# New instruction prices for the planner that orders all five queues, a price for a wait on one's own engine, turns of VectorE and GpSimd, and the sign of the first MLP's weights set on VectorE

## The chip, the cores and the metric

The kernel runs on one core of a Trainium2 chip. The metric is the device time of one execution in microseconds (us), from the first to the last instruction and the little that lies around it. Five engines work side by side, each through a queue of its own in a fixed order: TensorE (PE in the rows, with its weight loads as PEld), VectorE (DVE), ScalarE (ACT), GpSimd (POOL) and SyncE (SP), which only issues transfers.

## The reference

Top-32 attention over 4 batches, 8 heads, 576 positions and head size 64, then two MLPs in a row over the 2304 resulting tokens, 512 to 2048 to 512 each. All inputs are float32 or wider; the kernel reads the MLPs' weights as pairs of 32-bit words.

```python
scores = scale * np.matmul(q, k.transpose(0, 1, 3, 2))
kth = np.partition(scores, -top_k, axis=-1)[..., -top_k:-top_k + 1]
scores = np.where(scores >= kth, scores, -1000000000.0)
scores = scores - np.max(scores, axis=-1, keepdims=True)
attn = np.exp(scores); attn = attn / (np.sum(attn, axis=-1, keepdims=True) + 1e-09)
x = np.matmul(attn, v)            # then (batch, seq, heads * head_dim)
h = x @ w_in;   x = (np.maximum(h, 0.0) + np.log1p(np.exp(-np.abs(h)))) @ w_out     # first MLP
h = x @ w_in2;  y = (h - np.tanh(h)) @ w_out2                                      # second MLP
```

## The kernel before

Every large product is made from float16 pairs, a high part and a low part of each operand, with three matmuls for one (high by high, high by low, low by high).

Attention is cut into 144 tiles of 128 query rows by 576 scores. For each tile `front` makes the scores on TensorE and copies them to the tile `ssb` on ScalarE. `chain` finds the 32 largest of each row on VectorE: four MAX8 (eight largest values, into `m`) and between them three MATCH_REPLACE8 (write a very small number over those eight, into `x`), each of which needs the one before it; a MATCH_REPLACE8 stands in the trace behind a short MATCH_VALUE_LOAD. `exps`, `mask` and `turn` make the masked exponentials (ScalarE, VectorE, GpSimd), split them into `hl` (ScalarE high part, GpSimd low part) and send them through a transposing transfer to `pT`. `back` multiplies with the values into `px` and normalises (`x32`, `xs`). The chains of two neighbouring tiles are recorded in turns. There are three buffers each of `ssb` and `x`.

The MLPs run over chunks of 256 tokens (two smaller ones of 128). A chunk's first MLP can run when the 16 or more tiles that make its tokens are done. A step is an eighth of the inner width: `gemm1` (PSUM tile `h`), `act1` (ScalarE's softplus or tanh into `r`, for tanh a VectorE instruction more, ScalarE's `g` high part, GpSimd's scaled `r` and low part), `gemm2` (PSUM tiles `y`). In the rows `hinab`, `gsab` belong to the first MLP, `hinb`, `gsb` to the second.

The four weight matrices are turned into float16 pairs in the kernel, in 32 groups (8 of each matrix), the first MLP's 16 groups first. They lie early in the run, beside the first attention tiles. `weight_convert` (line 619) rebuilds magnitudes from the two words; `weight_split` (line 656) sets sign and scale and makes the pair. The tiles of these instructions are called `whi`, `wlo` and `xy` in the rows, after the place where the raw words lie: the rows with 128x1024 are groups in one piece, those with 128x256 are groups in four pieces. All 16 groups of the first MLP are in one piece, and 8 of the second MLP's. With `SGN[i]` "1" a group in one piece costs, in `weight_split`: VectorE one tensor_scalar that puts the scale under the sign bit, GpSimd two multiplications of 512 columns, ScalarE one copy to the high part, GpSimd two subtractions of 512 columns for the low part. With "0" (the `else` branch, there already): VectorE one scalar_tensor_tensor that joins sign and magnitude, ScalarE one activation with the scale to the high part, GpSimd one tensor_scalar of 1024 columns in place (`WSE` is "1"), and the same two subtractions.

No order of instructions is written by hand. The kernel's functions only record operations (class `Recorder`); at the end `order` (line 376) runs a list scheduler, `place` (line 309), over the whole program, five times with ranks improved between, takes the turn with the shortest plan, and issues the operations in that order. Each engine of the plan takes, at the time when it is free, the operation with the lowest rank among those that are ready; when none is ready it moves to the first that gets ready. For TensorE those ready for 500 ns are preferred. A duration comes from `price` (line 219), a delay between dependent operations from `close` (line 270): for another engine's result the producer's latency (100 to 350 ns), for a result of the same engine, or of a transfer, 0. `CON` (0.3) makes a VectorE operation that `two` (line 259) names (more than 8 elements, all inputs in SBUF, no MAX8 or MATCH_REPLACE8) 30% longer when GpSimd is busy at its start, and a GpSimd operation longer by 30% of its overlap with such a one. All of this is issued from one helper, so every row has its line, L402. The scheduler's plan is only an order: on the chip each engine works through its queue in that order and waits at its head for what is late.

Of the kernel before, what the change touches and what calls it, by code (L numbers as in the profile page):

```python
# [27 lines left out]
V2 = 'BD'  # L28
WSE = '1111'
PLAN = '01_23 01_23 01_23 01_23'  # L30
SGN = '1111'
PSB = '0000'
NRM = 'cccc'
EVL = 'AA'
HIC = 'AAAA'
CON = 0.3
SOFT = 1
NKT = 2
NQT = 2
# [98 lines left out]
class Recorder:  # L138
# [80 lines left out]
    def price(self, eng, method, a, k, outs, ins):  # L219
        out = outs[0]  # L220
        n = max(math.prod(x.shape[1:]) for x in outs + ins)
        if eng == "PE":
            cols = math.prod(out.shape[1:])
            if ins[0].dtype == F32:
                return 240 + cols * 4 / 2.4, 350.0
            return max(31.0, cols / 2.4 + 2.5), 350.0
        if eng == "SP":
            size = math.prod(out.shape) * mybir.dt.size(out.dtype)
            if "transpose" in method:
                return 1350.0, size / 164.0  # L230
            return 540.0, size / 330.0
        if eng == "ACT":
            if method == "copy":
                return 90 + 0.82 * n, 160.0
            c = 90 + 0.88 * n
            if len(a) > 2 and a[2] == AF.Exp:
                c += 200
            c += 70 * sum(isinstance(k.get(x), View) for x in ("bias", "scale"))
            return c + (95 if k.get("accum_out") is not None else 0), 160.0
        if eng == "DVE":  # L240
            if method == "max":
                return 705.0, 140.0
            if method == "match_replace":
                return 700.0, 140.0
            if n <= 8:
                return 400.0 if method == "scalar_tensor_tensor" else 120.0, 140.0
            if method == "tensor_reduce":
                return 300.0, 140.0
            far = any(isinstance(x, View) and x.ap.space == bass.MemoryType.PSUM for x in ins)
            if method in ("tensor_scalar", "tensor_copy"):  # L250
                return (70 + 1.1 * n if far else 100 + 0.58 * n), 140.0
            return (50 + 1.3 * n if far else 140 + 1.04 * n), 140.0
        if method == "memset":
            return 100 + 0.4 * n, 100.0
        if method == "tensor_scalar":
            return 270 + 0.84 * n, 100.0
        return 200 + 1.7 * n, 100.0

    def two(self, op):

# [9 lines left out]
    def close(self, op):  # L270
        op.i = len(self.ops)
        self.ops.append(op)

        def need(j):
            if j != op.i:
                o = self.ops[j]
                op.preds[j] = 0.0 if o.eng in (op.eng, "SP") else o.lat

        for mine, both in ((op.reads, False), (op.writes, True)):
            for g, (p0, p1, lo, hi) in mine:  # L280
                if not g.users or g.users[-1] != op.i:
                    g.users.append(op.i)
                for lst in (g.writes, g.reads) if both else (g.writes,):
                    for q0, q1, l, h, j in lst:
                        if q0 < p1 and p0 < q1 and l < hi and lo < h:
                            need(j)
        for g, (p0, p1, lo, hi) in op.writes:
            for lst in (g.reads, g.writes):
                lst[:] = [e for e in lst if not (p0 <= e[0] and e[1] <= p1 and lo <= e[2] and e[3] <= hi)]
            g.writes.append((p0, p1, lo, hi, op.i))  # L290
        for g, (p0, p1, lo, hi) in op.reads:
            g.reads.append((p0, p1, lo, hi, op.i))
# [16 lines left out]
    def place(self, edges, count, rank, margin, ring):  # L309

        ops = self.ops
        left = list(count)
        ready = [0.0] * len(ops)
        start, end = [0.0] * len(ops), [0.0] * len(ops)
        free = dict.fromkeys(("PE", "DVE", "ACT", "POOL", "SP"), 0.0)
        coming = {e: [] for e in free}
        avail = {e: [] for e in free}
        for o in ops:
            if not left[o.i]:
                heapq.heappush(coming[o.eng], (0.0, o.i))  # L320
        two, both = self.wide, 0.0
        done, busy = [], 0.0
        while True:
            best = None
            for e in free:
                if avail[e]:
                    t = free[e]
                elif coming[e]:
                    t = max(free[e], coming[e][0][0])
                else:  # L330
                    continue
                if best is None or t < best[0]:
                    best = t, e
            if best is None:
                break
            t, e = best
            while coming[e] and coming[e][0][0] <= t:
                r, i = heapq.heappop(coming[e])
                heapq.heappush(avail[e], (rank[i], i))
            i = None  # L340
            if margin.get(e):
                aside = []
                while avail[e]:
                    x = heapq.heappop(avail[e])
                    if ready[x[1]] <= t - margin[e]:
                        i = x[1]
                        break
                    aside.append(x)
                for x in aside:
                    heapq.heappush(avail[e], x)  # L350
            if i is None:
                i = heapq.heappop(avail[e])[1]
            o = ops[i]
            start[i] = t
            done.append(o)
            cost = o.cost
            if CON:
                if e == "DVE" and two[i]:
                    if free["POOL"] > t:
                        cost *= 1 + CON  # L360
                    both = t + cost
                elif e == "POOL" and both > t:
                    cost += CON * min(both - t, cost)
            end[i] = free[e] = t + cost
            if ring and e == "SP":
                busy = max(busy, t + 800) + o.lat
                end[i] = busy + 1000
            for j, lat in edges[i]:
                ready[j] = max(ready[j], end[i] + lat)
                left[j] -= 1  # L370
                if not left[j]:
                    heapq.heappush(coming[ops[j].eng], (ready[j], j))
        assert len(done) == len(ops)
        return start, end, done
# [31 lines left out]
def topk_attention_two_mlps(  # L406
# [249 lines left out]
    def weight_split(i, g, parts, used, ss):  # L656
# [8 lines left out]
        for st, cols in parts:  # L665
            low, high = st[:, :, 0], st[:, :, 1]
            w, hi, lo = high.bitcast(F32), whi[i][:, cols], wlo[i][:, cols]
            n = w.shape[1] // LSP if w.shape[1] > 512 else w.shape[1]
            if SGN[i] == "1":
                nc.vector.tensor_scalar(high, high, -0x80000000, s.bitcast(I32), op0=ALU.bitwise_and, op1=ALU.bitwise_or)  # L670
# [850 lines left out]
```

## Time and profile before

| | us |
|---|---|
| median of 3 runs | 1232.31 |
| lowest, highest | 1231.5, 1236.07 |
| the profiled execution, its own time | 1232.63 |
| its span, first to last instruction | 1230.9 |
| VectorE busy in the span | 1015.2 |
| TensorE busy in the span | 1001.5 |
| GpSimd busy in the span | 933.8 |
| ScalarE busy in the span | 906.7 |

The profile is of one execution. Busy times of an engine are the union of its instructions' spans. In the timeline an instruction's span runs some 80 ns into that of the next one on its engine, so the pace of an engine is read from one start to the next, not from the spans. A stretch given in us counts from the first instruction.

### The profile page before, as it was taken

The numbers are of one execution on the slowest core, as the hardware profiler recorded it, in microseconds if no ns is written. First come the engines' busy times: TensorE is split into PE (matmuls) and PEld (weight loads), VectorE is DVE, ScalarE is ACT, GpSimd is POOL, SyncE is SP. The second block draws the span as 40 slices with busy tenths as digits, with TensorE's granted clock in tenths as the row PEclk, the third lists the DMA queues.
The fourth block names the chain that finished last, engine by engine and source line by source line (L and its number), as shares of the span: only waits on it lengthen the run. The fifth ranks groups of instructions, "written<-read, shape, count | busy, mean of one in ns | idle before, by whom it ended". The sixth has DMA issues, their size and how long they took to land.

```text
span 1230.9 us, 27536 instructions
## 1 busy us (share of the span) xinstructions
PE 1001.5 (81%) x9832; PEld 791.0 (64%) x9832; DVE 1015.2 (82%) x2146; ACT 906.7 (74%) x1834; POOL 933.8 (76%) x1282
## 2 busy tenths in 40 slices
PE   2333323587897999888999999999997999999998
PEld 2222222476655876776678876887676768977974
DVE  4999999899998999999999999999898998710011
ACT  7988888867998897768876886799667766733332
POOL 4999998888987965866889868888795778743433
PEclk9999996698899989998999999999999999999999
DMA  8977888724687676634765644456464435210000
GB/s 281 275 231 223 209 220 218 189 76 95 125 177 183 143 177 119 129 73 93 147 128 127 115 93 94 93 117 131 99 132 99 80 74 95 49 23 18 2 3 25
DMA packets 322827, 153.16 MB, mean 124 GB/s; under 512 B 270208, under 2 KB 302464, under 8 KB 322688
## 3 DMA queue, kind: packets, MB, share of 16 engines
q1 hardware_dynamic: 322688, 151.39, 53.8%
q8 instruction: 77, 1.26, 0.4%
q14 instruction: 62, 0.51, 0.1%
HBM read 73.04 MB, written 15.37 MB: 72 GB/s over the span
## 4 chain that ended last, share of the span: by engine, by line
POOL 26%; DVE 24%; PE 23%; ACT 10%; issue 8%; DMA 7%; SPq 1%; POOLq 0%; DVEq 0%; ACTq 0%
PE h L402 11%; PE y L402 10%; DVE m L402 9%; DVE x L402 8%; POOL hl L402 6%; POOL wlo L402 5%; POOL g L402 3%; DMA pT<-hl 3%; POOL x L402 2%; POOL r L402 2%; POOL whi L402 2%; POOL nb L402 2%; ACT x L402 2%; ACT r L402 2%; DMA whi<-in_moe_w_in_dram 1%
## 5 line engine op out<-in xcount | busy, mean ns | idle before, releaser
L402 PE MATMUL h<-xy,whi 128*128 128x256 f16 (+1 forms) x2560 | 406.7, 266 | 4.7 <-DMA xy<-xs 1.7
L402 PEld LDWEIGHTS <-whi 128*128 128x128 f16 x3840 | 360.8, 99 | 67.4 <-issue 10.9
L402 PE MATMUL h<-xy,wlo 128*128 128x256 f16 (+1 forms) x1280 | 329.4, 266 | 0.0
L402 DVE MAX8 m<-x 128x8 f32<-128x576 f32 x432 | 320.4, 753 | 7.2
L402 POOL TENSOR_TENSOR hl<-x,hl 128x512 f16<-128x512 f32 (+1 forms) x288 | 214.6, 764 | 51.4 <-ACT hl L402 42.6
L402 DVE MATCH_REPLACE8 x<-m,x 128x576 f32<-128x576 f32 x288 | 213.4, 741 | 0.0
L402 PE MATMUL y<-g,whi 128*128 128x256 f16 (+1 forms) x1280 | 199.6, 263 | 9.2 <-ACT r L402 5.2
L402 PEld LDWEIGHTS <-wlo 128*128 128x128 f16 x1920 | 189.7, 99 | 25.5 <-issue 5.9
L402 PE MATMUL y<-whi,g 128*128 128x512 f16 x576 | 192.4, 379 | 2.0 <-DVE xy L402 1.5
L402 POOL TENSOR_TENSOR g<-r,g 128x512 f16<-128x512 f32 (+1 forms) x160 | 172.3, 1077 | 20.4 <-PE y L402 9.4
L402 PE MATMUL y<-g,wlo 128*128 128x256 f16 (+1 forms) x640 | 162.9, 263 | 0.0
L402 DVE SCALAR_TENSOR_TENSOR r<-h,hinb,r 128x512 f32<-128x512 f32 (+1 forms) x80 | 55.1, 689 | 124.5 <-ACT r L402 124.2
L402 ACT ACTIVATE x<-ssb,nb,tiny 128x576 f32<-128x576 f32 x144 | 124.3, 865 | 38.0 <-DVE m L402 20.0
L402 PE MATMUL px<-vhl,pT 128*128 128x65 f16 (+1 forms) x2240 | 102.3, 202 | 51.6 <-DMA pT<-hl 25.3
L402 PEld LDWEIGHTS <-pT 128*128 128x128 f16 (+1 forms) x2240 | 94.2, 106 | 72.0 <-DMA pT<-hl 33.8
L402 PE MATMUL s<-kT,qT 128*128 128x288 f16 x512 | 95.3, 315 | 50.0 <-ACT ssb L402 30.7
L402 PEld LDWEIGHTS <-g 128*128 128x128 f16 x864 | 83.1, 98 | 77.5 <-issue 2.1
L402 ACT CAST hl<-x 128x576 f16<-128x576 f32 x144 | 96.4, 670 | 33.7 <-POOL x L402 28.3
L402 DVE MAX8 m<-ssb 128x8 f32<-128x576 f32 x144 | 107.4, 746 | 5.1 <-ACT ssb L402 4.9
L402 PE MATMUL y<-wlo,g 128*128 128x512 f16 x288 | 109.1, 379 | 0.0
L402 DVE MATCH_REPLACE8 x<-m,ssb 128x576 f32<-128x576 f32 x144 | 106.7, 741 | 0.0
L402 POOL TENSOR_SCALAR r<-r,gsb 128x512 f32<-128x512 f32 (+1 forms) x80 | 52.2, 652 | 60.5 <-ACT g L402 58.3
(123 smaller groups left out, 1797.8 us busy)
## 6 DMA issues: line engine op xcount, KB each, us to landing
whi<-in_moe_w_in_dram SPq DMA_DIRECT2D x8, 1024.0 KB, 7.0
wlo<-in_moe_w_in_dram SPq DMA_DIRECT2D x6, 1024.0 KB, 7.0
vd<-vhl SPq DMA_DIRECT2D x16, 330.0 KB, 3.6
vhl<-vd SPq DMA_DIRECT2D x16, 330.0 KB, 3.3
kd<-kT SPq DMA_DIRECT2D x32, 160.0 KB, 2.3
whi<-in_moe_w_out_dram SPq DMA_DIRECT2D x5, 1024.0 KB, 5.7
wlo<-in_moe_w_out_dram SPq DMA_DIRECT2D x5, 1024.0 KB, 5.1
kT<-kd SPq DMA_DIRECT2D x32, 160.0 KB, 2.8
```

The costliest lines, as they stand in the source:

```text
L402: fn(*a, **k)
```

## The change

Four things are changed in the planner, and one in the program.

1. `price`: ScalarE's activations lose 10 ns, its Exp 155 ns more; MAX8 goes from 705 ns to 78 + 1.04 ns a column (677 ns for 576), MATCH_REPLACE8 from 700 to 659 ns; other VectorE operations and GpSimd's get new lines (a GpSimd subtraction of 512 columns goes from 1070 to 1101 ns, its one-column tensor_scalar from 271 to 330 ns, its multiplication of 576 from 1179 to 1360 ns).
2. `turn`, new: an operation that reads or overwrites what an earlier operation of the same engine wrote is ready only some time after that one's end: 116 ns on VectorE (196 ns if it is a MATCH_REPLACE8), 130 ns on ScalarE, 120 ns on GpSimd.
3. `CON` is 0.7 and works both ways: when a VectorE operation that `two` names or a GpSimd operation starts while the other engine is in one, both get longer by 0.7 of the overlap, and what depends on the one already running gets ready later.
4. `place` puts back an operation whose ready time has moved.
5. `SGN` is "0011": the 16 groups of the first MLP take the `else` branch of `weight_split`.

```diff
--- before.py
+++ after.py
@@ -28,12 +28,12 @@
 V2 = 'BD'
 WSE = '1111'
 PLAN = '01_23 01_23 01_23 01_23'
-SGN = '1111'
+SGN = '0011'
 PSB = '0000'
 NRM = 'cccc'
 EVL = 'AA'
 HIC = 'AAAA'
-CON = 0.3
+CON = 0.7
 SOFT = 1
 NKT = 2
 NQT = 2
@@ -232,29 +232,35 @@
         if eng == "ACT":
             if method == "copy":
                 return 90 + 0.82 * n, 160.0
-            c = 90 + 0.88 * n
+            c = 80 + 0.88 * n
             if len(a) > 2 and a[2] == AF.Exp:
-                c += 200
+                c += 45
             c += 70 * sum(isinstance(k.get(x), View) for x in ("bias", "scale"))
             return c + (95 if k.get("accum_out") is not None else 0), 160.0
         if eng == "DVE":
             if method == "max":
-                return 705.0, 140.0
+                return 78 + 1.04 * n, 140.0
             if method == "match_replace":
-                return 700.0, 140.0
+                return 60 + 1.04 * n, 140.0
             if n <= 8:
-                return 400.0 if method == "scalar_tensor_tensor" else 120.0, 140.0
-            if method == "tensor_reduce":
-                return 300.0, 140.0
+                return 350.0 if method == "scalar_tensor_tensor" else 80.0, 140.0
             far = any(isinstance(x, View) and x.ap.space == bass.MemoryType.PSUM for x in ins)
             if method in ("tensor_scalar", "tensor_copy"):
-                return (70 + 1.1 * n if far else 100 + 0.58 * n), 140.0
-            return (50 + 1.3 * n if far else 140 + 1.04 * n), 140.0
+                return (40 + 1.1 * n if far else 130 + 0.53 * n), 140.0
+            return (20 + 1.25 * n if far else 90 + 1.07 * n), 140.0
         if method == "memset":
-            return 100 + 0.4 * n, 100.0
+            return 200 + 0.4 * n, 100.0
         if method == "tensor_scalar":
-            return 270 + 0.84 * n, 100.0
-        return 200 + 1.7 * n, 100.0
+            return 330.0 if n <= 8 else 250 + 0.8 * n, 100.0
+        if method == "tensor_mul":
+            return (220 + 1.98 * n if n > 512 else 200 + 1.57 * n), 100.0
+        return 190 + 1.78 * n, 100.0
+
+    def turn(self, first, then):
+
+        if then.eng == "DVE":
+            return 196.0 if then.calls[0][0].__name__ == "match_replace" else 116.0
+        return {"ACT": 130.0, "POOL": 120.0}.get(then.eng, 0.0)
 
     def two(self, op):
 
@@ -271,10 +277,16 @@
         op.i = len(self.ops)
         self.ops.append(op)
 
-        def need(j):
+        def need(j, after):
             if j != op.i:
                 o = self.ops[j]
-                op.preds[j] = 0.0 if o.eng in (op.eng, "SP") else o.lat
+                if o.eng == "SP":
+                    lat = 0.0
+                elif o.eng == op.eng:
+                    lat = self.turn(o, op) if after else 0.0
+                else:
+                    lat = o.lat
+                op.preds[j] = max(lat, op.preds.get(j, 0.0))
 
         for mine, both in ((op.reads, False), (op.writes, True)):
             for g, (p0, p1, lo, hi) in mine:
@@ -283,7 +295,7 @@
                 for lst in (g.writes, g.reads) if both else (g.writes,):
                     for q0, q1, l, h, j in lst:
                         if q0 < p1 and p0 < q1 and l < hi and lo < h:
-                            need(j)
+                            need(j, lst is g.writes)
         for g, (p0, p1, lo, hi) in op.writes:
             for lst in (g.reads, g.writes):
                 lst[:] = [e for e in lst if not (p0 <= e[0] and e[1] <= p1 and lo <= e[2] and e[3] <= hi)]
@@ -318,7 +330,7 @@
         for o in ops:
             if not left[o.i]:
                 heapq.heappush(coming[o.eng], (0.0, o.i))
-        two, both = self.wide, 0.0
+        two, now = self.wide, {"DVE": None, "POOL": None}
         done, busy = [], 0.0
         while True:
             best = None
@@ -336,7 +348,12 @@
             t, e = best
             while coming[e] and coming[e][0][0] <= t:
                 r, i = heapq.heappop(coming[e])
-                heapq.heappush(avail[e], (rank[i], i))
+                if ready[i] > t:
+                    heapq.heappush(coming[e], (ready[i], i))
+                else:
+                    heapq.heappush(avail[e], (rank[i], i))
+            if not avail[e]:
+                continue
             i = None
             if margin.get(e):
                 aside = []
@@ -354,13 +371,17 @@
             start[i] = t
             done.append(o)
             cost = o.cost
-            if CON:
-                if e == "DVE" and two[i]:
-                    if free["POOL"] > t:
-                        cost *= 1 + CON
-                    both = t + cost
-                elif e == "POOL" and both > t:
-                    cost += CON * min(both - t, cost)
+            if CON and (e == "POOL" or e == "DVE" and two[i]):
+                x, other = now["DVE" if e == "POOL" else "POOL"], "DVE" if e == "POOL" else "POOL"
+                if x is not None and free[other] > t:
+                    ov = CON * min(free[other] - t, cost)
+                    cost += ov
+                    free[other] += ov
+                    end[x] += ov
+                    for j, lat in edges[x]:
+                        ready[j] = max(ready[j], end[x] + lat)
+            if e in now:
+                now[e] = i if e == "POOL" or two[i] else None
             end[i] = free[e] = t + cost
             if ring and e == "SP":
                 busy = max(busy, t + 800) + o.lat
```

## Rows read from the trace of the kernel before

**Rows 1.** The page: the span in 40 slices, busy tenths of TensorE and of VectorE

```profile
PE   2333323587897999888999999999997999999998
...
DVE  4999999899998999999999999999898998710011
```

**Rows 2.** Windows: stretch, length, busy PE, PEld, DVE, ACT, POOL (instructions), granted clock, transfers

```profile
77.00:231.00 154.00, 50.45 (x415) 38.55 (x414) 145.73 (x294) 133.58 (x268) 148.03 (x160) 0.88 0.79 212
231.00:690.00 459.00, 407.87 (x4038) 325.28 (x4038) 438.27 (x955) 365.73 (x776) 373.71 (x543) 0.95 0.61 129
690.00:1077.00 387.00, 370.50 (x3919) 297.90 (x3917) 355.72 (x743) 289.70 (x578) 297.54 (x441) 0.99 0.48 97
1077.00:1231.00 154.00, 149.23 (x1311) 112.17 (x1308) 18.49 (x37) 51.27 (x88) 56.95 (x74) 0.99 0.05 14
```

**Rows 3.** Timeline of ScalarE: first softplus of the first and of the second chunk

```profile
241.94 0.66 ACT L402 ACTIVATE r<-h,hinab 128x512 f32<-128x512 f32 x1
...
383.88 0.69 ACT L402 ACTIVATE r<-h,hinab 128x512 f32<-128x512 f32 x1 [0.45 <-PE h L402]
```

**Rows 4.** Waits of TensorE in 231 to 690: us in total, times, longest

```profile
PE s L402 <- ACT ssb L402: 12.5, 9, 3.4
PE px L402 <- DMA pT<-hl: 9.6, 11, 3.6
```

**Rows 5.** Timeline of VectorE (start us, span us, what): two stretches of the chains

```profile
26.55 0.76 DVE L402 MAX8 m<-ssb 128x8 f32<-128x576 f32 x1
27.34 0.09 DVE L402 MATCH_VALUE_LOAD x<-m,ssb 128x8 f32 x1
27.42 0.74 DVE L402 MATCH_REPLACE8 x<-m,ssb 128x576 f32<-128x576 f32 x1
28.20 0.76 DVE L402 MAX8 m<-x 128x8 f32<-128x576 f32 x1
28.88 0.87 DVE L402 SCALAR_TENSOR_TENSOR vhl<-v,tiny,vhl 128x640 f16<-128x640 f32 x1
...
29.73 0.75 DVE L402 MATCH_REPLACE8 x<-m,x 128x576 f32<-128x576 f32 x1
30.39 0.75 DVE L402 MAX8 m<-ssb 128x8 f32<-128x576 f32 x1
...
1070.77 0.76 DVE L402 MAX8 m<-x 128x8 f32<-128x576 f32 x1
1071.56 0.09 DVE L402 MATCH_VALUE_LOAD x<-m,x 128x8 f32 x1
1071.64 0.74 DVE L402 MATCH_REPLACE8 x<-m,x 128x576 f32<-128x576 f32 x1
1072.42 0.76 DVE L402 MAX8 m<-x 128x8 f32<-128x576 f32 x1
```

**Rows 6.** Groups by form: xcount, then busy us, mean ns of one, idle before

```profile
L402 POOL TENSOR_TENSOR whi<-whi 128x512 f32<-128x512 f32 x26 | 33.1, 1291 | 0.1
L402 DVE SCALAR_TENSOR_TENSOR whi<-whi 128x1024 int32<-128x1024 int32 x13 | 19.8, 1522 | 3.2 <-ACT whi L402 2.7 <-POOL hl L402 0.5
L402 DVE TENSOR_SCALAR whi<-whi,tiny 128x1024 int32<-128x1024 int32 x13 | 14.0, 1079 | 0.5
L402 POOL TENSOR_SCALAR r<-r,gsab 128x512 f32<-128x512 f32 x64 | 45.4, 709 | 34.9 <-ACT g L402 32.1 <-PE h L402 2.4
```

**Rows 7.** Timeline of GpSimd and VectorE: weight operations alone, and side by side from 118.86

```profile
30.72 1.04 POOL L402 TENSOR_TENSOR whi<-whi 128x512 f32<-128x512 f32 x1
...
77.84 0.76 DVE L402 TENSOR_SCALAR wlo<-wlo,tiny 128x1024 int32<-128x1024 int32 x1
...
118.86 2.11 POOL L402 TENSOR_TENSOR wlo<-wlo 128x512 f32<-128x512 f32 x1
...
118.86 1.21 DVE L402 SCALAR_TENSOR_TENSOR whi<-whi 128x1024 int32<-128x1024 int32 x1
119.99 1.26 DVE L402 SCALAR_TENSOR_TENSOR xy<-xy 128x256 int32<-128x256 int32 x1
```


## The prediction

> **What bounds the kernel now.** First the 40 slices [rows 1]. TensorE's digits are 2 and 3 for seven slices (to 215 us), mostly 8 and 9 after that, and 9 nearly to the end; VectorE is at 8 or 9 from the second slice to the thirty-fourth and almost idle from the thirty-sixth. So there are two limits in turn: VectorE (with GpSimd beside it) decides when TensorE gets MLP work at all, and after that TensorE has to work off its matmuls, 407.9 + 370.5 + 149.2 = 927.6 us from 231 on [rows 2]. The windows by stage put numbers to it [rows 2]. In 77 to 231 VectorE is busy 145.7 and GpSimd 148.0 of 154 us, TensorE 50.5: the weights and the first 16 tiles of attention. In 231 to 690 TensorE is busy 407.9 of 459, so 51.1 us are lost there, with VectorE busy 438.3. In 690 to 1077 TensorE lacks only 16.5 us of 387, and in 1077 to 1231 4.8 of 154, with no attention left. The marks of the middle stage are the first softplus of chunk one at 241.9 and of chunk two at 383.9, the latter 0.45 us after waiting for its matmuls [rows 3]: between them TensorE ran out of chunks, and the chunk came when VectorE was through with its tiles. The two longest of its waits in 231 to 690 are for attention's own steps, 12.5 us before the scores (`ssb`) and 9.6 us before the product with the values (`pT`) [rows 4]. An earlier chunk two shortens the run as long as TensorE has nothing else; later, time given back to VectorE falls into TensorE's queue and is worth little.
>
> **The waits between VectorE's own steps (prices and `turn`).** The pace is read from start to start [rows 5]. A MAX8 followed by work that doesn't need it: 28.20 to 28.88, 0.68 us; a MATCH_REPLACE8 followed by another tile's MAX8: 29.73 to 30.39, 0.66. Where the next needs the one before, the MAX8 at 26.55 lets the next start at 27.34 (0.79) and the MATCH_REPLACE8 at 27.42 at 28.20 (0.78); the last pairs of the run, from 1070.77 and 1071.64, show the same 0.79 and 0.78. Exact differences over the whole timeline are 0.116 us after a MATCH_REPLACE8 and 0.136 after a MAX8. Counting the timeline's neighbours without idle time between them: 211 MATCH_REPLACE8 are followed by a MAX8 that waits (first and last as above) and 70 by one that doesn't; 159 MAX8 are followed by a MATCH_VALUE_LOAD that waits (first and last as above) and 91 by one that doesn't. By stage there are 15 and 7 waiting pairs before 231, 87 and 64 in 231 to 690, 109 and 88 after 690. So the free time inside VectorE's busy time is 15 x 0.116 + 7 x 0.136 = 2.7 us, then 10.1 + 8.7 = 18.8 us, then 12.6 + 12.0 = 24.6 us; some 46 us of 1072.
>
> The old plan took these pairs for free, so it had no reason to part them. The new one makes the second of a pair ready 116 or 196 ns late; an operation of lower rank that is ready then goes between. VectorE is busy 95% of 231 to 690 [rows 2], so as a rule one is queued, and I take three quarters as removed: a choice, between none (all of the other ready work needs the same chain) and all. It costs something too: the operation that steps in is 0.66 us long where 0.12 was the wait, so a chain's next step comes up to 0.54 us later, while the engine as a whole gains.
>
> One rule speaks against this part. The Trainium skill, in VectorE: DVE Perf Modes, section "The DRAIN you can't avoid", says that the pipeline is emptied after every VectorE operation and that a chain with waits takes the same time as one without. By that an order with other work in between would free nothing, and this part of the sum would be 0. The rows disagree here: 0.66 to 0.68 us against 0.78 to 0.79 for the same shapes [rows 5].
>
> **The sign of the first MLP's weights.** Per group of 1024 columns VectorE's tensor_scalar (mean 1079 ns) becomes a scalar_tensor_tensor over two tiles, for which the same shape in `weight_convert` shows 1522: +0.44, times 16 groups +7.1 us of VectorE. GpSimd's two multiplications of 512 (1291 each, 2.58) become one tensor_scalar of 1024. Its 1024-column form isn't in the trace; the 512 form takes 709 [rows 6], so it lies between 0.71 and 2 x 0.71 = 1.42. I take 1.42, since GpSimd's operations grow about with their columns; GpSimd then saves 1.16, times 16 = 18.6 us (29.9 at the other end). ScalarE's copy becomes one activation of the same columns; I cost it at 0, since ScalarE is busy 133.6 of 154 us [rows 2]; at 0.1 us each it would be 1.6 us if that cover were gone. GpSimd's wait for ScalarE only moves: before, its subtractions waited for the copy; now the scaling in place waits until ScalarE has read the tile, with attention's subtractions for `hl` queued behind it, and VectorE's last steps behind those. I cost that at 0, between -1.1 and +1.1 us a group (a pass of ScalarE).
>
> Which of +7.1 and -18.6 counts? Both engines are full in 77 to 231, and they hold each other up: alone the multiplication takes 1.04, but the one at 118.86, begun with VectorE's scalar_tensor_tensor, takes 2.11, and the VectorE operation that follows at 119.99 takes 1.26 for 256 columns [rows 7]. One works while the other stands. So I add what the group holds of both, taken alone: before 0.76 + 2 x 1.04 = 2.84 us, after 1.13 (118.86 to 119.99) + 1.42 = 2.55 [rows 7]. That is -0.29, times 16 = -4.6 us. No DMA moves with this branch.
>
> **The turns of VectorE and GpSimd (`CON`) and the other prices.** They add and remove no instruction. With 0.7 both ways the plan comes nearer to the rows (a multiplication of 1.04 that takes 2.11), so operations are less often put where they can't start yet, and TensorE's waits [rows 4] can shrink. I count nothing for it; the bounds are the 22.1 us of [rows 4] gained and as much lost, since another order may also be a worse one.
>
> **The sum.** Before 231: -4.6 and three quarters of 2.7, together -6.6, of which I keep -5, since part of it meets GpSimd's own queue. 231 to 690: three quarters of 18.8 is -14; it comes through one to one, because TensorE has 51.1 us without work there and waits for the chunks. After 690: three quarters of 24.6 is 18 us of VectorE, but TensorE is idle only 16.5 of 387 us; I keep -3. Together -22: the profiled execution took 1232.63 us (span 1230.9), so 1210.6; the median of the runs shown is 0.3 lower, which makes 1210. At their favourable ends the terms are -21 (-18.6 - 2.7), -19 and -16.5 (all of TensorE's idle time), together -56; they hardly come at once, and half of the way there, -39, is 1194, the good end of the forecast.
>
> **The rivals.** *TensorE is the limit everywhere.* Then the middle term is 0: chunk two comes earlier, but the 51 us are lost to waits at the head of TensorE's queue and to its lower granted clock (0.95 in that stage [rows 2]), and the time before 231 alone counts: 1232.6 - 5 = 1228. For it: 95 to 97% busy in the last two stages. Against it: the empty stretch before 383.9 [rows 3]. The case in which interleaving frees nothing, with the same time, belongs here, with little weight after [rows 5].
> *VectorE pays for the sign.* In 77 to 231 the join costs VectorE its full +7.1 us and GpSimd's relief isn't used, since VectorE has the longer queue; the first chunk's softplus comes after 249 instead of 241.9, TensorE is full afterwards and everything moves: 1232.6 + 7.1 = 1240. It decides if VectorE, not the pair of them, ends the stage: VectorE busy over 97% there with GpSimd well below 90%. For it: VectorE is already at 95%. Against it: GpSimd is at 96%, and the two hold each other up [rows 7].
> *The plan's change doesn't act*: no independent operation is ready, the counts of waiting pairs stay above 150 and 110. That gives 1228 again.
>
> **How the numbers follow.** The forecast, 1194 to 1226, gets 0.55. A larger gain, below 1194, gets 0.07. No change within 0.5% (1226 to 1238.5; about what a measurement of this kernel can tell from no change) gets 0.20: the first and third rivals. Slower by over 0.5% gets 0.18, the second rival and orders that happen to be worse. So faster 0.62, same 0.20, slower 0.18. The range 1194 to 1243 leaves some 0.07 below and 0.08 above.
>
> **What would show it.** The waiting pairs fall from 211 and 159 to about 55 and 40, and VectorE's busy time by some 25 to 30 us net of the +7; GpSimd's falls by about 20 us before 231. The first softplus comes near 237, that of chunk two near 370; TensorE's idle time in the middle stage falls from 51 towards 37 us; VectorE ends near 1045 instead of 1073. I am wrong if pairs vanish and chunk two still comes at 384, or if VectorE's busy share before 231 rises while chunk one comes later.

## The result and the profile after

The changed kernel takes 1215.12 us (median of 4 runs, 1214.0 to 1215.4); the kernel before in the runs beside it 1232.43. The ratio of the mean times is 0.9852, 95% interval 0.9832 to 0.9873; by the medians it is 17.3 us faster. The forecast was 1210. The profiled execution took 1215.22 us, its span is 1213.4, 17.5 less than before.

The page of after, busy times and the slices of TensorE and VectorE (for [rows 1]):

```profile
PE 997.0 (82%) x9832; PEld 788.5 (65%) x9832; DVE 991.4 (82%) x2146; ACT 899.0 (74%) x1834; POOL 921.4 (76%) x1266
...
PE   2242333677797979998999999999998999999998
...
DVE  4989899999999999899999999989899889610021
```

VectorE is busy 23.8 us less (991.4 against 1015.2). The windows of after, same columns and stretches as [rows 2]:

```profile
77.00:231.00 154.00, 52.03 (x418) 38.26 (x419) 137.50 (x286) 133.27 (x267) 142.34 (x153) 0.97 0.82 216
231.00:690.00 459.00, 413.68 (x4137) 331.44 (x4137) 441.52 (x1003) 366.78 (x787) 379.13 (x554) 0.95 0.60 130
690.00:1077.00 387.00, 377.12 (x4059) 305.95 (x4057) 337.98 (x716) 288.58 (x582) 300.76 (x442) 1.00 0.50 98
1077.00:1213.40 136.40, 132.00 (x1075) 96.00 (x1072) 15.23 (x28) 44.93 (x73) 49.07 (x62) 1.00 0.04 11
```

TensorE lacks 45.3 us in 231 to 690 instead of 51.1, and 9.9 in 690 to 1077 instead of 16.5. Where on the way the time was won is read from the first softplus of each chunk of 256 tokens. The timeline of ScalarE, after (chunks one, two, three, four and seven):

```profile
238.15 0.69 ACT L423 ACTIVATE r<-h,hinab 128x512 f32<-128x512 f32 x1 [0.94 <-PE h L423]
...
389.09 0.67 ACT L423 ACTIVATE r<-h,hinab 128x512 f32<-128x512 f32 x1
...
499.54 0.69 ACT L423 ACTIVATE r<-h,hinab 128x512 f32<-128x512 f32 x1
...
620.91 0.67 ACT L423 ACTIVATE r<-h,hinab 128x512 f32<-128x512 f32 x1
...
982.35 0.69 ACT L423 ACTIVATE r<-h,hinab 128x512 f32<-128x512 f32 x1
```

The same of before, for chunks three, four and seven (one and two stand in [rows 3]):

```profile
491.51 0.69 ACT L402 ACTIVATE r<-h,hinab 128x512 f32<-128x512 f32 x1
...
624.22 0.69 ACT L402 ACTIVATE r<-h,hinab 128x512 f32<-128x512 f32 x1 [1.32 <-PE h L402]
...
999.11 0.69 ACT L402 ACTIVATE r<-h,hinab 128x512 f32<-128x512 f32 x1
```

After against before: -3.8 us, +5.2, +8.0, -3.3, and -16.8 at chunk seven. So 4 us are won in the weights' stage and lost again by chunk two; all that lasts is won between 500 and 1000 us. Such marks move by themselves: in the five profiled executions whose queues have the order of the kernel before (before itself and runs 7, 8, 10 and 11 below, which differ from it only later), chunk one starts between 241.69 and 244.30. The first of the five differences is hardly more than that. The last MAX8 of the run starts at 1054.98 instead of 1072.42 [rows 5], 17.4 earlier, which is the whole gain.

The order that does it, in the timeline of VectorE after (two stretches, as in [rows 5]):

```profile
31.23 0.76 DVE L423 MAX8 m<-ssb 128x8 f32<-128x576 f32 x1
31.90 0.08 DVE L423 MATCH_VALUE_LOAD x<-m,x 128x8 f32 x1
31.96 0.75 DVE L423 MATCH_REPLACE8 x<-m,x 128x576 f32<-128x576 f32 x1
32.62 0.08 DVE L423 MATCH_VALUE_LOAD x<-m,ssb 128x8 f32 x1
32.69 0.74 DVE L423 MATCH_REPLACE8 x<-m,ssb 128x576 f32<-128x576 f32 x1
33.35 0.75 DVE L423 MAX8 m<-x 128x8 f32<-128x576 f32 x1
...
1054.21 0.74 DVE L423 MATCH_REPLACE8 x<-m,x 128x576 f32<-128x576 f32 x1
1054.98 0.76 DVE L423 MAX8 m<-x 128x8 f32<-128x576 f32 x1
```

The two tiles' chains now alternate step by step: whatever follows a MAX8 or a MATCH_REPLACE8, a MATCH_VALUE_LOAD too, starts 0.66 to 0.67 us after it, where a waiting pair takes 0.77 to 0.79 (the last two rows are one that is left). Counted as in the prediction, the waiting pairs fall from 211 to 44 and from 159 to 39.

The weights' groups by form, after (for [rows 6]; count, busy us, mean ns, idle before):

```profile
L423 DVE SCALAR_TENSOR_TENSOR whi<-whi 128x1024 int32<-128x1024 int32 x21 | 33.6, 1598 | 6.5 <-ACT whi L423 6.5
L423 POOL TENSOR_SCALAR wlo<-wlo,tiny 128x1024 f32<-128x1024 f32 x8 | 12.0, 1504 | 2.6 <-ACT whi L423 2.4
L423 POOL TENSOR_SCALAR whi<-whi,tiny 128x1024 f32<-128x1024 f32 x8 | 11.8, 1470 | 6.3 <-ACT whi L423 6.1
```

GpSimd's new form takes 1.47 to 1.50 us on average and now waits for ScalarE ahead of it, 8.5 us in all. The prediction took 1.42 for one alone; the one at 129.88 us, beside which VectorE has nothing but steps of the chains, takes 1.19 and the next starts 1.14 us after it.

### The profile page after: what moved, and what is told of

Same layout as the page of the kernel before. It is cut to its first block, busy times and chain, and to the rows that moved or that the text cites. A ratio compares the mean times of both kernels' runs of the same rounds, so it can differ in the third digit from the quotient of the medians.

```text
span 1213.4 us, 27486 instructions
## 1 busy us (share of the span) xinstructions
PE 997.0 (82%) x9832; PEld 788.5 (65%) x9832; DVE 991.4 (82%) x2146; ACT 899.0 (74%) x1834; POOL 921.4 (76%) x1266
## 5 line engine op out<-in xcount | busy, mean ns | idle before, releaser
L423 PE MATMUL h<-xy,whi 128*128 128x256 f16 (+1 forms) x2560 | 404.7, 265 | 10.7 <-ACT r L423 5.0
L423 PEld LDWEIGHTS <-whi 128*128 128x128 f16 x3840 | 361.2, 99 | 69.9 <-issue 12.6
L423 DVE MAX8 m<-x 128x8 f32<-128x576 f32 x432 | 315.3, 748 | 1.5
L423 POOL TENSOR_TENSOR hl<-x,hl 128x512 f16<-128x512 f32 (+1 forms) x288 | 217.7, 772 | 46.9 <-ACT hl L423 38.6
L423 PEld LDWEIGHTS <-qT 128*128 128x128 f16 x512 | 50.9, 106 | 91.1 <-issue 61.7
```

Source lines behind the costliest of these rows:

```text
L423: fn(*a, **k)
```

## The experiments

The question was which part makes the gain, and whether it comes through VectorE's time at all. Ratios are to the kernel before in runs on the same chip, with 95% intervals. "Last MAX8" is its start in the profiled execution.

**1. The branch alone.** Edit, on the kernel before:

```diff
-SGN = '1111'
+SGN = '0011'
```

> The kernel before with the sign of the first MLP's weights set on VectorE (SGN 0011), planner as before. Theory of the prediction (the pair of VectorE and GpSimd bounds the weights' stage): -4.6 us, 1226 to 1230. Rival that VectorE alone pays: +7, about 1239. Rival that the branch is the whole of the gain: 1215.

Measured: 1245.62 us, ratio 1.0097 (1.0076 to 1.0118): 12 us slower, outside all three expectations. Chunk one starts at 240.7, chunk two at 394.5 (383.9 before), last MAX8 at 1085.1. VectorE is busy 1023.3 us, 8.1 more; GpSimd 922.9, 10.9 less. Attention's own steps place the loss: of its 576 MAX8 the 128th starts at 343.3 us (332.2 before), 11.1 later, and the last 12.6 later. So nearly all of it arises by then.

**2. The planner alone.** Edit, on the changed kernel:

```diff
-SGN = '0011'
+SGN = '1111'
```

> The changed kernel with the sign as before (SGN 1111): prices, waits on one's own engine and turns alone. Theory: most of the gain stays, 1218 to 1222. Rival that the branch is the whole of the gain: 1231. Rival that VectorE pays for the sign: below 1212.

Measured: 1218.66 us, ratio 0.9879 (0.9856 to 0.9902). The planner alone makes about four fifths of the gain (ratio 0.9879 against 0.9852). The branch, which costs 12 us in the old plan, costs nothing that shows in the new one; whether it gains there can't be told, since the two intervals overlap.

**3. Without the wait's price.** Edit, on the changed kernel:

```diff
-                    lat = self.turn(o, op) if after else 0.0
+                    lat = 0.0
```

> The changed kernel with the wait between dependent operations of one engine priced at nothing again, all else as changed. Theory: the waiting pairs come back (over 150 MATCH_REPLACE8 to MAX8, over 110 MAX8 to MATCH_VALUE_LOAD), VectorE is busy 25 us more, and 10 us or more of the gain are lost: 1225 or more. Rival that the other prices and the turns of VectorE and GpSimd make the gain: 1213 to 1218 with the pairs back.

Measured: 1246.98 us, ratio 1.011 (1.007 to 1.015). The waiting pairs are 264 and 224, more than before the change. Its page:

```profile
PE 1009.0 (81%) x9832; PEld 794.9 (64%) x9832; DVE 1025.6 (82%) x2146; ACT 908.6 (73%) x1834; POOL 919.2 (73%) x1266
```

VectorE is busy 34 us longer than with the price (991.4). The whole gain is gone. That it is slower than the kernel before by 1.1% is about what the branch costs by itself in a plan without the price (run 1: 1.0%), so nothing here says that the new prices and turns are worse than the old ones.

**4. The old rule for VectorE and GpSimd side by side.** Edit, on the changed kernel: `CON` 0.3 and the old block in `place` instead of

```diff
-            if CON and (e == "POOL" or e == "DVE" and two[i]):
+            if CON:
+                if e == "DVE" and two[i]:
+                    if free["POOL"] > t:
+                        cost *= 1 + CON
...
```

> The changed kernel with the old rule for VectorE and GpSimd side by side (30%, one way), all else as changed. Theory: the turns add nothing of their own, 1211 to 1219. Rival that they make the gain: 1225 or more.

Measured: 1217.14 us, ratio 0.987 (0.985 to 0.989), pairs 48 and 34. The turns of VectorE and GpSimd add nothing that these runs can tell.

**5. The wait's price alone.** Edit, on the kernel before: the function `turn` is added, `need` takes `after`, and

```diff
+                if after and o.eng == op.eng:
+                    lat = self.turn(o, op)
```

> The kernel before with nothing but the wait between dependent operations of one engine priced (turn): old prices, old rule for VectorE and GpSimd side by side, sign as before. Theory (the wait's price makes the gain by itself): the waiting pairs fall below 60 and 60, 1215 to 1221. Rival that it needs the other prices: 1227 or more.

Measured: 1219.39 us, ratio 0.988 (0.9851 to 0.991), pairs 29 and 27, last MAX8 at 1059.1. The wait's price is enough by itself, with old prices, old turns and the old sign. Chunk two comes early here, at 371.26 us, and in run 2 late, at 391.79; the last MAX8 starts at the same time in both, within 0.7 us:

```profile
371.26 0.67 ACT L410 ACTIVATE r<-h,hinab 128x512 f32<-128x512 f32 x1
...
1059.10 0.76 DVE L410 MAX8 m<-x 128x8 f32<-128x576 f32 x1
```

and in run 2

```profile
391.79 0.67 ACT L423 ACTIVATE r<-h,hinab 128x512 f32<-128x512 f32 x1
...
1058.46 0.76 DVE L423 MAX8 m<-x 128x8 f32<-128x576 f32 x1
```

So when chunk two starts doesn't decide when attention ends.

**6. The wait's price on VectorE alone.** Edit, on the changed kernel:

```diff
-        return {"ACT": 130.0, "POOL": 120.0}.get(then.eng, 0.0)
+        return 0.0
```

> The changed kernel with the wait priced on VectorE alone, at nothing on ScalarE and GpSimd. Theory (VectorE's pairs are what counts): 1213 to 1219. Rival that waits of ScalarE and GpSimd carry a part: 1222 or more.

Measured: 1221.54 us, ratio 0.990 (0.9873 to 0.9928), pairs 60 and 44. Between the two expectations; most of the gain is VectorE's. The interval just touches that of the full change (0.9832 to 0.9873), so the other engines' price may be worth some 5 us, which one pair of runs doesn't settle.

So the price of the wait between dependent steps makes the gain. Does it act by the time that it frees on VectorE? The next runs take time away with every queue's order kept to the instruction.

**7 and 8. VectorE's time taken away in place.** Edit, on the kernel before (the planner prices the full width; tiles 30 to 84, or 89 to 143):

```diff
-            return lambda: nc.vector.max(m[:, 8 * i : 8 * i + 8], src)
+            return lambda: [o.calls[0][1].__setitem__(1, src[:, 0 : S // 4].ap) for o in [nc.vector.max(m[:, 8 * i : 8 * i + 8], src)] if i == 3 and CUT[0] <= st.i < CUT[1]]
```

> The kernel before, its order kept to the instruction; only the last MAX8 of tiles 30 to 84 (the stretch from 320 to 650 us) reads 144 columns instead of 576, so these tiles' threshold comes from a quarter of the scores. VectorE saves 55 x 0.45 = 25 us. Theory of the prediction (before 690 TensorE waits for the chunks): most of it comes through, 1208 to 1213. Rival that TensorE is the limit everywhere: 1229 or more.

> The same cut in tiles 89 to 143 (from 680 us to the end of attention) instead: 25 us of VectorE. Theory of the prediction (after 690 TensorE is full and the time falls into its queue): 1228 or more, some 3 us gained. Rival that the end of attention sets the end of the run to the last: 1208 to 1213.

Measured: in the middle 1230.89 us, ratio 0.9974 (0.9954 to 0.9994); late 1230.52, ratio 0.9966 (0.995 to 0.9981). Of 25 us 3.6 and 3.9 come through, in the middle as little as late. In the middle that meets the number of the rival (TensorE the limit everywhere), which run 10 tries; late it meets the theory's number. The window of the first of the two and VectorE's waits in it:

```profile
231.00:690.00 459.00, 411.17 (x4059) 327.66 (x4057) 418.41 (x959) 368.28 (x783) 375.85 (x547) 0.94 0.61 130
...
DVE r L402 <- ACT r L402: 16.1, 20, 2.2
DVE ssb L402 <- ACT x L402: 9.9, 11, 3.2
```

The same waits in the kernel before:

```profile
DVE r L402 <- ACT r L402: 5.4, 9, 1.3
DVE ssb L402 <- ACT x L402: 4.6, 6, 2.2
```

VectorE's busy time falls from 438.3 [rows 2] to 418.4 and TensorE's stays within 3 us; VectorE waits instead, 10.7 us more for the second MLP's tanh and 5.3 more for the exponentials.

**9. The same time, known to the planner.** Edit, on the kernel before: the shorter MAX8 of run 7 is recorded as such, and

```diff
-                return 705.0, 140.0
+                return 57 + 1.125 * n, 140.0
```

> The kernel before with the same short last MAX8 in tiles 30 to 84 as in cut_mid, but known to the planner (a MAX8 of 144 columns priced 219 instead of 705 ns), so that all queues are ordered anew. In cut_mid, with every order kept, 25 us of VectorE gave 3.6 us. Theory now (time freed on VectorE counts only when the plan lets TensorE's queue move up with it): 1210 to 1220. Rival (VectorE's time in the middle isn't a limit at all): 1228 to 1232.

Measured: 1241.38 us, ratio 1.0045 (1.0034 to 1.0057). Slower with less to do, outside both expectations. The waiting pairs are 252 and 233 instead of 211 and 159: a planner that takes them for free makes more or fewer of them with an edit that has nothing to do with them. That the added pairs cost the 5 us isn't shown; the whole order is another.

The plans made so far can be set side by side. The five with the price on VectorE's waits (the full change and runs 2, 4, 5 and 6) have 29 to 60 and 27 to 44 waiting pairs and ratios of 0.985 to 0.990; the four without it (before and runs 1, 3 and 9) 202 to 264 and 159 to 233, and 1 to 1.011. Within a kind the orders differ by 6 and by 14 us, but the kinds don't overlap, so the gain isn't one lucky order.

**10. TensorE's time taken away in place.** Edit, on the kernel before, at the end of a burst of matmuls of the two chunks of batch 1:

```diff
-        self.close(op)
+        self.close(op); [c[1].__setitem__(k, c[1][k][:, 0 : c[1][k].shape[1] // 2]) for c in op.calls[1::3] for k in (0, 2) if self.half]
```

> The kernel before, its order kept to the instruction; in the two chunks of batch 1 (their MLPs lie between 490 and 880 us) one of the three products of every matmul group, the one with the activations' low part in the first product and with a low part in the second, covers half of its columns: 384 matmuls of 256 columns and 64 of 512 are halved, 27 us less of TensorE. Theory now (with the orders kept TensorE's queue sets the pace): 1207 to 1215. Rival (attention's steps set it, TensorE only fills): 1226 or more.

Measured: 1234.44 us, ratio 0.9984 (0.9972 to 0.9997). TensorE's busy time falls by 24.4 us (977.1 against 1001.5), the run by 1.5. TensorE's time in this stretch isn't the limit either.

**11. Both at once.** Edit: runs 7 (tiles 59 to 113) and 10 together.

> The kernel before, its order kept to the instruction, with both kinds of shortening in the same stretch: the last MAX8 of tiles 59 to 113 reads 144 columns (25 us less of VectorE between 490 and 880 us; the threshold of these tiles comes from a quarter of the scores) and the halved matmuls of pe_cut (27 us less of TensorE there). Apart they gave 3.6 and 1.5 us. Theory now (VectorE and TensorE are limits at the same time, each hides what the other gains): together far more than the sum, 1210 to 1220. Rival (a third thing, GpSimd, ScalarE or a round trip through all of them, sets the pace): about the sum, 1228 to 1232.

Measured: 1232.0 us, ratio 0.9981 (0.9969 to 0.9993). The two-limits theory falls; the rival's number is met. Windows 490 to 690 and 690 to 880 of this run:

```profile
490.00:690.00 200.00, 166.97 (x1900) 136.86 (x1898) 181.67 (x430) 151.86 (x316) 161.24 (x234) 0.95 0.57 116
690.00:880.00 190.00, 180.86 (x1968) 144.05 (x1967) 173.26 (x395) 151.69 (x305) 147.23 (x232) 0.99 0.51 106
```

Over the 390 us TensorE is busy 347.8, VectorE 354.9, ScalarE 303.6 and GpSimd 308.5: none is full, and yet the last MAX8 starts at 1071.1 instead of 1072.4. TensorE's longest waits there:

```profile
PE px L402 <- DMA pT<-hl: 13.5, 14, 3.8
PE s L402 <- ACT ssb L402: 10.4, 10, 2.9
PE px L402 <- DVE n L402: 8.1, 4, 4.3
```

The first two are for attention's own round trips, through four engines and the transposing transfer. The third is for something else: a buffer `px`, which the products with the values share with column sums, and out of which VectorE reads such a sum (`n`) for a scale.

**12. VectorE's queue alone planned anew.** Edit, on the kernel before: after the plan is made, the other four queues are chained in their order and `place` runs again with the waits on VectorE priced:

```diff
+        for e in ("PE", "ACT", "POOL", "SP"):
+            line = [o for o in best[1] if o.eng == e]
+            kept += zip(line, line[1:])
...
+                succ[j].append((o.i, max(lat, o.late.get(j, 0.0))))
```

> The kernel before with the queues of TensorE, ScalarE, GpSimd and SyncE kept to the instruction; VectorE's queue alone is planned again, with the waits between its dependent operations priced. Theory now (two limits): the waiting pairs fall below 100 and 80 and VectorE stands idle for the time instead; the end moves by 3 to 8 us, 1227 to 1232. Rival (the gain of the change is VectorE's queue alone): 1215 to 1221.

Measured: 1226.39 us, ratio 0.9934 (0.9916 to 0.9952): 8 us, with pairs down to 41 and 42, last MAX8 at 1066.1. Neither expectation is met to the number, the theory's nearly: VectorE's queue by itself makes about half of what the price makes when all queues are planned with it (run 5: 15 us, with ScalarE and GpSimd priced too). Planning VectorE's queue once more without the price wasn't run, so it isn't shown that the 8 us are all the price's. By the counts and waits of the prediction the pairs removed free some 36 us of VectorE (170 x 0.116 + 117 x 0.136, an estimate); 8 us of them come through, about a fifth, against about a seventh in runs 7 and 8.

The starts of the last MAX8 and the spans of these runs go together; seven of the fourteen kernels:

| profiled execution | last MAX8 | span | difference |
|---|---|---|---|
| before | 1072.4 | 1230.9 | 158.5 |
| after | 1055.0 | 1213.4 | 158.4 |
| sign_only | 1085.1 | 1243.6 | 158.5 |
| no_turn | 1093.4 | 1251.0 | 157.6 |
| turn_on_before | 1059.1 | 1217.1 | 158.0 |
| cut_late | 1067.0 | 1226.1 | 159.1 |
| dve_reordered | 1066.1 | 1224.9 | 158.8 |

What follows attention takes 157.6 to 159.1 us in all fourteen, whatever came before. The end of the run is the end of attention plus this.

## Why the prediction was right, and where its steps were wrong

The direction, the part of the change that makes the gain, and about the size hold: -22 was forecast, -17.4 came, 1215.1 lies within the forecast's own range, and the wait's price does it (runs 3 and 5). The way from freed time to the end of the run was wrong, in two steps whose errors offset each other; that the size came near is partly luck.

*The waits on VectorE*: right. The pairs, 44 and 39, were forecast at about 55 and 40; VectorE's busy time fell by 23.8 us (25 to 30 forecast). The rule of the Trainium skill, in VectorE: DVE Perf Modes, section "The DRAIN you can't avoid", by which a chain with waits takes the same time as one without, is measured there on copies, and the section adds that an operation which isn't held back starts earlier. It doesn't hold for these instructions here: 0.66 to 0.67 us against 0.77 to 0.79, and run 12, which changes VectorE's order alone, is 0.66% faster.

*The sign, -4.6 us in 77 to 231*: this step failed too. Chunk one came at 238.15 us (237 forecast), but in the old plan the branch costs 12 us, more than the 7.1 of the rival that VectorE pays. The loss shows not at chunk one, as the rival had it (240.7), but in attention's own steps (11.1 us at 343 us) and at chunk two (394.5). In the new plan it costs nothing that shows. VectorE's share was sized about rightly (8.1 us more busy in run 1, 7.1 forecast); GpSimd's busy time falls by 10.9 in run 1, of 18.6 forecast. The two durations that were added up as alone weren't both so: the 1.13 us of VectorE at 118.86 had GpSimd beside it [rows 7], and GpSimd's form takes 1.19 alone, not 1.42. Adding up what a group holds of both engines doesn't tell the end; why the old plan loses 12 us and the new one none stays open.

*231 to 690, -14 "one to one"*: this step failed. Chunk two came at 389.1 instead of the 370 forecast while the pairs vanished, which the prediction itself had named as a sign of being wrong; and 25 us freed in place in this stretch give 3.6 (run 7). TensorE hadn't run out of chunks ahead of chunk two: its slices from 246 to 369 us read 8, 7, 8 and 9 [rows 1]. An early chunk two isn't worth its time either: run 5 has it at the 370 forecast and ends no earlier than run 2, which has it 20 us later. "Waits for a chunk" was read as "waits for VectorE"; but VectorE at 95% busy wasn't what set attention's pace with the orders kept, as run 7 shows.

*After 690, -3, "falls into TensorE's queue"*: this step failed the other way. TensorE at 96% busy isn't the limit: 24 us of it taken away between 490 and 880 us give 1.5 (run 10). VectorE's time is worth as little late as in the middle, 3.9 of 25 us (run 8), and yet all of the lasting gain is won between 500 and 1000 us. The two errors offset each other: the prediction had most of it before 690, the chip has -3.3 at chunk four and -16.8 at chunk seven.

*TensorE's waits* [rows 4]: the prediction counted nothing for a better order of the other queues. Run 12 against run 5 points to about half: 8 us with VectorE's queue alone, 15 with all (and with ScalarE and GpSimd priced too). After the change the same two waits are:

```profile
PE s L423 <- ACT ssb L423: 16.2, 8, 7.1
...
PE px L423 <- DMA pT<-hl: 3.4, 4, 1.8
```

The second falls from 9.6 to 3.4, the first rises by 3.7.

What stays open: which round trip sets attention's pace when the orders are kept. Runs 7, 8, 10 and 11 exclude VectorE's and TensorE's busy time, singly and together, in the stretches tried. So how the priced wait makes attention end sooner, beyond the part that is VectorE's time, isn't shown. That it is queues waiting at their heads for one another fits the waits and that no engine is full, but GpSimd's and ScalarE's time wasn't taken away, so it is argued and not shown.

## What to carry to other kernels

An engine that is 95% busy need not be what sets the pace: shorten its instructions in place, with all orders kept, before counting its time as the run's. Where queues are planned by a list scheduler, price the wait between dependent instructions of one engine; left at nothing, it comes back in numbers that vary with every other edit, and an edit is then judged by the order that it happens to get (run 9: less work, 5 us slower). And look for the mark that moves with the end, here the last MAX8, before dividing the run into stages with limits of their own.

## What was not expected of the hardware

The mean granted clock of TensorE says little of the time here: of the runs of the kernel before beside run 9, one at 0.912 took 1235.96 us and one at 0.978 took 1236.86. In the profiled executions the means differ above all by 77 to 231, where TensorE is busy some 50 of 154 us and half speed (the low level, 1.2 GHz) costs little: there the granted clock is 0.88 before [rows 2], with a mean of 0.962 over the span, and 0.53 in run 7, with a mean of 0.917, and chunk one starts only 2.4 us later in run 7 (244.30). From 231 to 490 the two are alike, 0.93 and 0.92.
